# Packed attention with routed experts: another order in the first two batches of a one-core kernel

## The chip, the cores and the metric

One core of one Trainium2 chip. The time is the device time of one execution in microseconds (us), median of several runs. Engines are named as in the profile: PE (TensorE matmul) with PEld (its weight loads), DVE (VectorE), ACT (ScalarE), POOL (GpSimd), SP (SyncE, which here only issues DMAs). PE, DVE, ACT, POOL and SP each take their instructions in the order in which the program emits them; between engines only semaphores order the work.

## The reference

```python
def sm_attn(qq, kk, vv):
    s = scale * np.matmul(qq, kk.transpose(0, 1, 3, 2))
    a = np.exp(s - np.max(s, axis=-1, keepdims=True))
    a = a / (np.sum(a, axis=-1, keepdims=True) + 1e-09)
    return np.matmul(a, vv)
p_packed = sm_attn(p, k, v)              # 32 packed rows a head
out = sm_attn(q, p_packed, p_packed)     # 8 batches, 8 heads, 576 rows, 64 wide
x = out.transpose(0, 2, 1, 3).reshape(4608, 512)
logits = normalized(x) @ normalized(expert_emb).T / tau     # 8 experts
expert_idx = np.argmax(logits, axis=1)
gate_w = softmax(logits)[chosen]
out[mask] = gate_w[mask] * (np.maximum(x[mask] @ w1[e], 0) @ w2[e])   # for each expert e
```

q, k, v are 8 x 8 x 576 x 64, p is 8 x 8 x 32 x 64, w1 is 8 x 512 x 1024 and w2 is 8 x 1024 x 512, all fp32.

## The kernel before

The 8 batches run one after another, overlapped. For each batch the kernel packs keys and values into 32 rows a head (key scores, exponential, pack product), scores the queries against the packed rows (att2's softmax), and **guesses one expert for the whole batch** from the sum of the packed rows' logits (`guess`, the "choice": DVE's max and index, then a register load on the issuing engine). It loads that expert's w1 and w2 and runs the expert layer with it. Rows that another expert should have had are counted and redone at the end in a loop that is entered only if there are any.

The attention output is never formed: since it is attention weights (AT) times packed rows, the kernel multiplies packed rows by w1 once (`w1_rows`, `rows_w1`: the tile G) and the hidden layer is G times AT. The routing logits and squared norms come from a product of AT with the packed rows and their logits (ppx, `route`, L679). For the fp32r products tiles are split in a high and a low half (ACT casts the high half, POOL or DVE subtracts: `split`, `split_w2`, `split_g`), and each product is three passes (PASSES). For batch 0 the first half of the hidden layer runs unsplit on fp32.

`ffn` is one batch's expert layer as a generator that yields after each group of products: for batch 0 two w1 row products (L843) and 8 hidden products of the first half of the rows (L875), 8 of the second half, 8 steps of the last 64 rows (L902), then four row blocks c of 8 steps each (L920, three 128x512 products a step). After every yield a hand-written PLAN says what of other generators is emitted: "q" is the next part of `begin` (the head), "s" one step of batch 0's softmax (in the order ORDS), "G" one split of G, "a" one step of batch 1's attention (`att_main(1)`), "w" one split of a w2 tile, "r" one step of batch 0's `route`, "g" one step of batch 0's `gates`. PLAN's entry 0 is emitted before ffn starts, entry k after its k-th yield. When batch 1's routing is done (`x.lg` is set), `w1_rows(1)` is emitted between the steps of the last row block (c = AHEAD = 3).

ENG says for batch 0 which of the softmax steps S0 S1 N0 N1 L0 L1 (subtract the maximum, normalize, low half; for the two halves of the rows) and which of the four splits of G go to POOL ("p") rather than DVE ("v"). All later batches use DVE.

PSUM is kept in rotating banks: three "pf" (hidden and output products), two double "pb" (scores, routing, w1_rows), one "pc". Loads go out on SP's queue, some of the head's on ACT's, and for batch 1 on w1 and w2 on POOL's. An output copy (`store`, L1209: ACT scales by the gate) for the row block before is emitted at the third step of the next block; batch 0's first only at the second block.

Names: kn, vn, qn: the head's whole-tile loads of batch 0; kn1, ny: keys and packed queries of batch 1; wy: ny scaled and doubled (L1152); T, Tw: packed rows turned; flip: a DVE transpose of a key or query tile (L276, L281); rows_split: the high and low halves of ppx; L721: the counts.

Of the kernel before, what the change touches and what calls it, by code (L numbers as in the profile page):

```python
# [25 lines left out]
def kernel(  # L26
# [63 lines left out]
    def rsqrt(x, y, tag, eng=nc.vector):  # L90
# [3 lines left out]
            out=i, in0=x.bitcast(I32), scalar1=1, scalar2=None, op0=ALU.logical_shift_right  # L94
        )
        yield
        nc.vector.tensor_scalar(
            out=i, in0=i, scalar1=-1.0, scalar2=float(0x5F3759DF), op0=ALU.mult, op1=ALU.add
# [29 lines left out]
    def embeddings():  # L128

        emb_sb = sb.tile([E, DM], F32, name="emb_sb", tag="st", bufs=2)  # L130
# [300 lines left out]

    def att1(x, nat, tight=False):
# [3 lines left out]
        def queries():  # L436
            for r in range(NPR):
                x.qT[r] = flip(nat(NPR + r), False)
                yield
# [40 lines left out]
        def pack_slowly():  # L480
# [23 lines left out]
            yield from queries()  # L504
            yield from rows_main()

        def rows_main():
            for g in range(NG):
                rows_split(x, g)
# [5 lines left out]
            logits_split(x)  # L515
# [41 lines left out]
    def att2(x, after=None, first=False, b1=False):  # L557

        def eng(name, hf):
            i = ("S0", "S1", "N0", "N1", "L0", "L1").index(name + str(hf))  # L560
            return nc.gpsimd if first and ENG[i] == "p" else nc.vector

# [169 lines left out]
    def gates(x):  # L732
        lg, ss = x.lg, x.ss
        y = sm.tile([P, NC5], F32, name="gy", tag="gy", bufs=1)
        for n, _ in enumerate(rsqrt(ss, y, "g")):
            if n % 3 == 2:
                yield
# [91 lines left out]
    def ffn(x, store, late=False, after=None, end=False):  # L829
# [63 lines left out]
        for hf in range(2):  # L893
            for f in range(NF):
                if late and hf == 0 and f % 4 == 0:
                    yield from rows_w1(f // 4)
                yield from hidden(hf, f)
# [83 lines left out]
    def att_main(b):  # L981
# [7 lines left out]
        second = att2(x, keys_main(b + 1) if b else None, b == 0, b < 1)  # L989
        if b:  # L990
            for _ in range(3):
                yield next(second)
            load_w2(x, x.e, nc.gpsimd)
        yield from second
# [7 lines left out]
    def begin():  # L1002
# [9 lines left out]
        vn = [load_v(0, g, nc.scalar) for g in range(NG)]  # L1012
        nc.scalar.dma_start(itau, tau.broadcast_to([P, 1]))
        qn = [load_whole(q[0], g) for g in range(NG)]
        ny = sm.tile([P, NG, D], F32, name="pn", tag="pn")
        nc.sync.dma_start(ny, p[1].rearrange("(g h) j d -> (h j) g d", g=NG))
        kn1 = [load_whole(k[1], g) for g in range(NG)]
# [7 lines left out]
        def warm(n):  # L1025
# [3 lines left out]
            for _ in range(n):  # L1029
                nc.tensor.matmul(pt[:, :P], fill, fill, start=True, stop=True)  # L1030
# [10 lines left out]
        for g in range(NG):  # L1041
            x.s1[g] = turn_bank()
            for e in range(2):
                kt = flip(kn[g], True, e)
                for hf in range(2):
                    quarters(x.s1[g], pw[:, 1, g, e], kt, lambda c: head(g, c), hf, hf, e)
            if g == 0:
                for _ in range(3):
# [364 lines left out]
```

## Time and profile before

| | us |
|---|---|
| median of 3 runs | 460.34 |
| lowest and highest | 458.28, 461.69 |
| the profiled execution | 458.36 |
| its span, first to last instruction | 456.8 |
| PE busy | 434.9 (95%) |
| DVE busy | 302.9 (66%) |
| ACT busy | 204.9 (45%) |
| POOL busy | 142.6 (31%) |

Mean granted TensorE clock 0.988 of full speed. Busy shares are averages over stages with different limits, and matmuls are pipelined, so a busy PE is not PE at its peak. What the change touches lies in the first quarter of the span: the head (0 to 30 us), batch 0's expert layer (28 to 94 us) and batch 1's attention beside it.

### The profile page before, as it was taken

How to read it: one execution, taken by the hardware profiler on the slowest of the kernel's cores; microseconds unless marked ns; L12 is line 12 of the kernel's file. 1: busy time of each engine (PE TensorE's matmuls, PEld its weight loads, DVE VectorE, ACT ScalarE, POOL GpSimd, SP SyncE). 2: the span in 40 equal slices, each digit the busy share in tenths (PEclk: the TensorE clock that was granted, in tenths of full speed). 3: DMA queues.
4: the chain of work that ended last, by engine and by line, in shares of the span. 5: the costliest groups of instructions: out<-in, count | busy, mean ns of one | idle time of the engine just before them, and what ended most of it. 6: DMA issues, size and time to landing. Idle time of an engine off the chain costs nothing.

```text
span 456.8 us, 10781 instructions
## 1 busy us (share of the span) xinstructions
PE 434.9 (95%) x3926; PEld 345.6 (76%) x3927; DVE 302.9 (66%) x925; ACT 204.9 (45%) x478; POOL 142.6 (31%) x181
## 2 busy tenths in 40 slices
PE   8678999969999999999999999999999999999993
PEld 6556767739788886879788896879788796879783
DVE  4557588536895588847894589847895589635500
ACT  2356732536325661375325651375325652466210
POOL 2352744221621345041521336040531336033200
PEclk9999999979999999999999999999999999999998
DMA  8799168963596686866598665876597524711022
GB/s 255 273 263 275 40 181 295 291 187 106 142 374 197 162 222 204 291 191 181 154 361 229 169 190 199 295 200 180 156 347 229 151 54 154 268 30 24 13 53 47
DMA packets 39869, 87.12 MB, mean 191 GB/s; under 512 B 11769, under 2 KB 19193, under 8 KB 39809
## 3 DMA queue, kind: packets, MB, share of 16 engines
q1 hardware_dynamic: 31248, 56.52, 44.4%
q0 software_dynamic: 7840, 29.36, 17.5%
q8 instruction: 33, 0.54, 0.5%
q10 hardware_dynamic: 720, 0.48, 0.4%
q14 instruction: 28, 0.22, 0.2%
HBM read 76.89 MB, written 9.44 MB: 189 GB/s over the span
## 4 chain that ended last, share of the span: by engine, by line
PE 84%; DVE 6%; ACT 4%; DMA 2%; issue 1%; POOL 1%; SPq 0%; ACTq 0%; DVEq 0%; POOLq 0%
PE pf L920 36%; PE pf L875 22%; PE pf L902 6%; PE pt L679 6%; PE pt L253 3%; PE pt L808 2%; PE pt L374 2%; PE pt L357 2%; DMA pn<-in_p 1%; DMA out<-o 1%; DVE kt L276 1%; ACT p L342 1%; DVE hT L880 0%; DVE at L616 0%; PE pt L231 0%
## 5 line engine op out<-in xcount | busy, mean ns | idle before, releaser
L920 PE MATMUL pf<-w2s,hT 128*128 128x512 f32 (+1 forms) x792 | 189.2, 390 | 0.0
L920 PEld LDWEIGHTS pf<-w2s,hT 128*128 128x128 f32 x792 | 142.0, 188 | 38.3 <-issue 9.4
L784 POOL TENSOR_TENSOR w2s<-w2r,w2s 128x512 fp32r<-128x512 f32 x64 | 82.4, 1289 | 230.2 <-ACT w2s L783 226.3
L875 PE MATMUL pf<-AT,G 128*128 128x288 f32 x720 | 106.9, 302 | 0.7 <-DVE h L885 0.4
L875 PEld LDWEIGHTS pf<-AT,G 128*128 128x128 f32 x720 | 99.2, 191 | 6.7 <-issue 3.2
L880 DVE SCALAR_TENSOR_TENSOR hT<-pf,hT 128x224 fp32r<-128x224 f32 (+1 forms) x128 | 52.5, 415 | 36.3 <-ACT hT L879 36.1
L879 ACT ACTIVATE hT<-pf 128x224 fp32r<-128x224 f32 (+1 forms) x128 | 48.6, 385 | 49.5 <-PE pf L875 48.1
L783 ACT CAST w2s<-w2r 128x512 fp32r<-128x512 f32 x64 | 39.2, 616 | 2.1 <-issue 1.2
L1209 ACT ACTIVATE o<-pf,gate 128x512 f32<-128x512 f32 (+1 forms) x41 | 26.0, 635 | 30.6 <-PE pf L920 17.5
L695 ACT ACTIVATE at<-pt 128x512 f32<-128x512 f32 (+1 forms) x40 | 23.9, 597 | 34.1 <-DVE lg L688 33.2
L679 PEld LDWEIGHTS pt<-ppx,AT 128*128 128x128 f32 (+1 forms) x240 | 33.1, 177 | 5.3 <-ACT w2s L783 0.8
L679 PE MATMUL pt<-ppx,AT 128*128 128x264 f32 (+1 forms) x240 | 36.2, 287 | 0.4 <-ACT at L695 0.4
L902 PE MATMUL pf<-w2r,h 128*64 128x256 f32 x256 | 34.3, 390 | 0.0
L822 DVE TENSOR_TENSOR G<-pt,G 128x512 fp32r<-128x512 f32 x28 | 18.9, 690 | 17.9 <-ACT G L821 17.9
L688 DVE TENSOR_REDUCE lg<-pt 128x8 f32<-128x16 f32 (+1 forms) x40 | 6.6, 165 | 33.1 <-PE pt L679 33.0
L595 ACT ACTIVATE st<-st 128x576 f32<-128x576 f32 (+1 forms) x17 | 11.2, 660 | 31.1 <-DVE st L592 30.4
L902 PEld LDWEIGHTS pf<-w2r,h 128*64 128x64 f32 x256 | 15.6, 136 | 9.8 <-issue 4.1
L281 DVE STREAM_TRANSPOSE kt<-nat 128x576 f32<-128x576 f32 x28 | 21.3, 764 | 0.0
L773 POOL DMA_DIRECT2D w2r<-in_moe_w x28 | 19.7, 710 | 0.0
L746 ACT ACTIVATE lg<-lg 128x40 f32<-128x40 f32 x8 | 1.9, 237 | 39.6 <-DVE lg L742 39.6
L622 ACT CAST AT<-at 128x576 fp32r<-128x576 f32 x16 | 10.8, 673 | 19.6 <-DVE at L616 19.6
L821 ACT CAST G<-pt 128x512 fp32r<-128x512 f32 x28 | 15.9, 588 | 7.4 <-DVE G L822 4.8
(181 smaller groups left out, 483.8 us busy)
## 6 DMA issues: line engine op xcount, KB each, us to landing
nat<-in_q SPq DMA_DIRECT2D x112, 140.0 KB, 3.4
w1t<-in_moe_w POOLq DMA_DIRECT2D x14, 1024.0 KB, 6.7
w2r<-in_moe_w POOLq DMA_DIRECT2D x28, 512.0 KB, 9.9
nat<-in_k SPq DMA_DIRECT2D x96, 140.0 KB, 3.1
vn<-in_v SPq DMA_DIRECT2D x46, 192.0 KB, 4.5
out<-o SPq DMA_DIRECT2D x124, 64.0 KB, 2.2
nat<-in_k SPq DMA_DIRECT2D x4, 576.0 KB, 6.0
w1t<-in_moe_w SPq DMA_DIRECT2D x4, 512.0 KB, 5.7
```

The source lines that it names most:

```text
L281: nc.vector.transpose(kt.rearrange("p (c i) -> p c i", i=32), t)
L679: nc.tensor.matmul(pt[:r, 512 * g : 512 * g + XW], AT[:, a, g, c * P : c * P + r], x.ppx[:, m, g], start=(i == 0), stop=(i == 2),)
L695: nc.scalar.activation(scr[:r, :, : HB * D], ptv[:r, :, 0 : HB * D], AF.Square, accum_out=ss[:r, c : c + 1])
L773: queue.dma_start(t, w2e[:, 2 * i : 2 * i + 2, :])
L783: nc.scalar.copy(t[:, 0], raw)
L784: nc.gpsimd.tensor_tensor(out=t[:, 1], in0=raw, in1=t[:, 0].bitcast(F32), op=ALU.subtract)
L875: nc.tensor.matmul(pf[:, :HS], w, r, start=(n == 0), stop=(n == len(ops) - 1))
L879: nc.scalar.activation(hT[:, 0, f, cs], pf[:, :n], AF.Relu)
L880: nc.vector.scalar_tensor_tensor(out=hT[:, 1, f, cs], in0=pf[:, :n], scalar=0.0, in1=hT[:, 0, f, cs].bitcast(F32), op0=ALU.max, op1=ALU.su ...
L902: nc.tensor.matmul(pf[64 * hf : 64 * hf + 64, :256], h4[:, f], x.w2r[f // 2][:, f % 2, hf * 256 : hf * 256 + 256], start=(f == 0), stop=(f ...
L920: nc.tensor.matmul(pf[:, :w], hT[:, a, f, c * P : (c + 1) * P], x.w2s[f][:, m, at : at + w], start=(f == 0 and i == 0), stop=(f == NF - 1 ...
L1209: nc.scalar.activation(o[:, :w], pf[:, :w], AF.Copy, scale=x.gate[:, c : c + 1])
```

## The change

In the head: a tiny exponential (`seen`) is ACT's first instruction after the first load's issue, so the activation table is loaded there. The embeddings' Square is emitted before tau's load, rsqrt's first step after the third key flip, and the Newton steps later. The shift and multiply of rsqrt become one operation. The packed queries and keys of batch 1 (ny, kn1) are loaded behind the first exponentials, with ny in a buffer of the tag "p1". wy's scaling is emitted before batch 0's choice is drained rather than after batch 0's scores. The warm-up is 4 products of 512 columns instead of 13 of 128.

Around batch 0's layer: batch 1's key scores come behind the first w1 rows. The second w1 rows are emitted before the fourth hidden product instead of before the fifth. N1 and L1 of batch 0 go to POOL, and N0, N1 and L1 of batch 1 (ENG1). Batch 0's gate Newton steps go to POOL. Batch 1's query flips leave its attention generator and get a letter of their own ("d"); its choice, w1 load and query scores come directly after the packed rows, its w2 load and the splits of ppx after them; PLAN is rewritten.

```diff
         i = sm.tile(list(x.shape), I32, name="rq_i", tag=f"rq_i{tag}", bufs=1)
         nc.vector.tensor_scalar(
-            out=i, in0=x.bitcast(I32), scalar1=1, scalar2=None, op0=ALU.logical_shift_right
-        )
-        yield
-        nc.vector.tensor_scalar(
-            out=i, in0=i, scalar1=-1.0, scalar2=float(0x5F3759DF), op0=ALU.mult, op1=ALU.add
+            out=i, in0=x.bitcast(I32), scalar1=-0.5, scalar2=float(0x5F3759DF),
+            op0=ALU.mult, op1=ALU.add,
         )
         yield
...
     def embeddings():
 
+        seen = sm.tile([1, 1], F32, name="seen")
+        nc.scalar.activation(seen, ones[:1], AF.Exp)
         emb_sb = sb.tile([E, DM], F32, name="emb_sb", tag="st", bufs=2)
...
+    def all_queries(x, nat):
+        for r in range(NPR):
+            x.qT[r] = flip(nat(NPR + r), False)
+            yield
+
     def att1(x, nat, tight=False):
...
         def queries():
-            for r in range(NPR):
-                x.qT[r] = flip(nat(NPR + r), False)
-                yield
+            yield from all_queries(x, nat)
...
             nc.vector.tensor_copy(x.T, pu[:, 0 : NG * P])
-            yield from queries()
-            yield from rows_main()
-
-        def rows_main():
-            for g in range(NG):
-                rows_split(x, g)
             yield
             pt = pc.tile([P, 512], F32, name="pu", tag="pu")
             row_logits(x, pt)
             logits_out(x, pt)
             yield
-            logits_split(x)
...
-    def att2(x, after=None, first=False, b1=False):
+    def att2(x, after=None, first=False, b1=False, eng1="vvvvvv"):
 
         def eng(name, hf):
             i = ("S0", "S1", "N0", "N1", "L0", "L1").index(name + str(hf))
-            return nc.gpsimd if first and ENG[i] == "p" else nc.vector
+            return nc.gpsimd if (ENG if first else eng1)[i] == "p" else nc.vector
...
-        for n, _ in enumerate(rsqrt(ss, y, "g")):
+        for n, _ in enumerate(rsqrt(ss, y, "g", nc.gpsimd if x is bat[0] else nc.vector)):
...
             for f in range(NF):
-                if late and hf == 0 and f % 4 == 0:
-                    yield from rows_w1(f // 4)
-                yield from hidden(hf, f)
+                if late and hf == 0 and f == 0:
+                    yield from rows_w1(0)
+                if late and hf == 0 and f == 3:
+                    ahead, now = rows_w1(1), hidden(hf, f)
+                    for part in (ahead, now, ahead):
+                        next(part)
+                        yield
+                    yield from now
+                    drain(ahead)
+                else:
+                    yield from hidden(hf, f)
...
-        second = att2(x, keys_main(b + 1) if b else None, b == 0, b < 1)
+        second = att2(x, keys_main(b + 1) if b else None, b == 0, b < 1, ENG1 if b == 1 else "vvvvvv")
         if b:
             for _ in range(3):
                 yield next(second)
             load_w2(x, x.e, nc.gpsimd)
+            if b == 1:
+                yield
+                assert hasattr(bat[0], "lg")
+                for g in range(NG):
+                    rows_split(x, g)
+                    yield
+                logits_split(x)
         yield from second
...
         vn = [load_v(0, g, nc.scalar) for g in range(NG)]
+        next(emb_gen)
         nc.scalar.dma_start(itau, tau.broadcast_to([P, 1]))
         qn = [load_whole(q[0], g) for g in range(NG)]
-        ny = sm.tile([P, NG, D], F32, name="pn", tag="pn")
-        nc.sync.dma_start(ny, p[1].rearrange("(g h) j d -> (h j) g d", g=NG))
-        kn1 = [load_whole(k[1], g) for g in range(NG)]
...
-                nc.tensor.matmul(pt[:, :P], fill, fill, start=True, stop=True)
+                nc.tensor.matmul(
+                    pt, fill, fill.unsqueeze(1).broadcast_to([P, 4, P]), start=True, stop=True
+                )
...
                 kt = flip(kn[g], True, e)
+                if g and not e:
+                    next(emb_gen)
...
-            if g == 0:
-                for _ in range(3):
-                    next(emb_gen)
...
         key_exp(x, 1)
+        ny = sb.tile([P, S], F32, name="ny", tag="p1", bufs=2)[:, : NG * D]
+        ny = ny.rearrange("p (g d) -> p g d", g=NG)
+        nc.sync.dma_start(ny, p[1].rearrange("(g h) j d -> (h j) g d", g=NG))
+        kn1 = [load_whole(k[1], g) for g in range(NG)]
+        next(emb_gen)
+        next(emb_gen)
         p1_evac(x, 0, pt, 0)
         nc.vector.reciprocal(itau, itau)
-        next(emb_gen)
         key_sum(x, 0)
...
         nc.scalar.copy(x.Tw, pu[:, : NG * P])
+        wy = sb.tile([P, 2, NG, 2 * D], F32, name="wy", tag="w2s", bufs=NF)
+        nc.gpsimd.tensor_scalar(
+            out=wy[:, 0].rearrange("p g (t d) -> p g t d", t=2),
+            in0=ny.unsqueeze(2).broadcast_to([P, NG, 2, D]),
+            scalar1=SCALE, scalar2=None, op0=ALU.mult,
+        )
         drain(g_guess)
...
-    WARM = 13
+    WARM = 4
...
-    ENG = "pppvpvppvp"
+    ENG = "ppppppppvp"
+    ENG1 = "vvppvp"
...
     PLAN = (
-        "qsssqsssssssqsqssqsssqs", "s", "s", "G", "s", "G", "s", "s", "s", "sG",
-        "G", "", "aq", "a", "aq", "as", "aq", "aws", "aqs", "awq",
-        "aw", "awr", "awr", "ar", "awr", "awr", "aw", "ar", "g", "gr",
-        "gr", "gr", "ga", "ga", "gra", "gr", "gra", "ra", "a", "a",
-        "a", "a", "a", "a", "ga", "a", "a", "aa", "a", "a",
-        "aa", "a", "aa", "a", "aa", "aa", "aa", "aa", "aa", "aa",
+        "qsssqsssssssqsqssssss", "qqs", "s", "s", "sG", "", "G", "", "s", "s",
+        "sG", "a", "aG", "aq", "a", "aqs", "aq", "aws", "aqs", "awq",
+        "aw", "awr", "adwr", "adr", "adwr", "adwr", "aw", "ar", "ag", "agr",
+        "agr", "agr", "ga", "ga", "gra", "gr", "gra", "ra", "a", "a",
+        "a", "a", "a", "a", "ga", "a", "aa", "a", "aa", "a",
+        "aa", "a", "aa", "a", "aa", "a", "aa", "a", "aa", "aa",
         "aa",
     )
...
+        asked = all_queries(bat[1], nat_main(1))
...
+                elif c == "d":
+                    next(asked, None)
```

(wy's scaling stood further down, right before its own transposes, in the same words.)

## Rows read from the trace of the kernel before

**Rows 1.** Waits of PE, whole span: us in total, times, longest us.

```profile
PE pt L253 <- DVE cnt L726: 3.7, 1, 3.7
PE pf L1159 <- POOL wy L1152: 1.9, 1, 1.9
```

**Rows 2.** Windows near 100 us: busy per engine, granted clock, DMA share, GB/s.

```profile
97.00:98.00 1.00, 0.00 (x0) 0.00 (x0) 0.59 (x1) 0.37 (x1) 0.00 (x0) 0.98 0.53 125
...
104.00:105.00 1.00, 1.00 (x6) 1.00 (x6) 0.12 (x1) 0.55 (x3) 0.00 (x0) 0.60 0.31 77
```

**Rows 3.** Timeline, 72 to 112 us: start, us, engine, line, [idle before <-releaser].

```profile
99.08 2.15 PE L253 MATMUL pt<-kt,pw 64*32 64x288 f32 x24 [3.71 <-DVE cnt L726]
...
101.16 5.86 PE L875 MATMUL pf<-AT,G 128*128 128x288 f32 x30
```

**Rows 4.** The timeline, 0 to 20 us.

```profile
1.22 5.34 PE L1030 MATMUL pf<-fill 128*128 128x128 f32 x26 [1.22 <-DVE mask L72]
...
5.64 1.28 ACT L134 ACT_TABLE_LOAD   x1 [5.51 <-DMA pn<-in_p]
...
6.54 4.35 PE L231 MATMUL pt<-kt,pw 32*32 32x288 f32 x64
6.93 0.63 ACT L134 ACTIVATE esq<-emb_sb 8x512 f32<-8x512 f32 x1
```

**Rows 5.** The timeline, 20 to 48 us.

```profile
22.43 0.67 POOL L592 TENSOR_TENSOR st<-st,mx 128x288 f32<-128x288 f32 x1 [5.92 <-DVE mx L586]
...
30.21 4.15 PE L875 MATMUL pf<-at,g 128*128 128x288 f32 x16 [0.68 <-ACT g L855]
...
35.41 1.42 PE L843 MATMUL pf<-w1t,tw 64*32 64x512 f32 x16 [1.06 <-DVE hT L880]
...
41.75 3.62 PE L875 MATMUL pf<-AT,G 128*128 128x288 f32 x24
```

**Rows 6.** The timeline of POOL, 47 to 76 us.

```profile
49.39 1.44 POOL L627 TENSOR_TENSOR AT<-at,AT 128x576 fp32r<-128x576 f32 x1
...
59.12 2.53 POOL L784 TENSOR_TENSOR w2s<-w2r,w2s 128x512 fp32r<-128x512 f32 x2 [0.66 <-ACT w2s L783]
61.65 1.44 POOL L268 TENSOR_TENSOR ppx<-pp,ppx 128x256 fp32r<-128x256 f32 x2
...
70.22 1.76 POOL L765 DMA_DIRECT2D w1t<-in_moe_w  x2 [2.83 <-DMA nat<-in_k]
71.97 2.83 POOL L773 DMA_DIRECT2D w2r<-in_moe_w  x4
```

**Rows 7.** The timeline, 48 to 72 us, PE and DVE.

```profile
52.50 0.65 PE L902 MATMUL pf<-w2r,h 128*64 128x256 f32 x4
...
61.62 1.66 PE L920 MATMUL pf<-w2s,hT 128*128 128x512 f32 x6
...
68.75 0.22 DVE L550 TENSOR_SCALAR sel<-ecol,gi 1x8 f32<-1x8 f32 x1
...
70.52 0.85 DVE L581 STREAM_TRANSPOSE st<-pt 128x288 f32<-128x288 f32 x2 [1.55 <-PE pt L253]
```

**Rows 8.** The timeline, 0 to 20 us, POOL's small steps.

```profile
8.16 0.18 POOL L107 TENSOR_TENSOR rq_t<-rq_h,rq_i 8x1 f32<-8x1 f32 x1 [0.18 <-DVE rq_i L97]
...
9.24 0.18 POOL L107 TENSOR_TENSOR rq_t<-rq_h,ery 8x1 f32<-8x1 f32 x1
```

**Rows 9.** The timeline, 72 to 112 us, DVE and PE.

```profile
75.58 0.69 DVE L592 TENSOR_TENSOR st<-st,mx 128x576 f32<-128x576 f32 x1
...
81.72 0.76 DVE L627 TENSOR_TENSOR AT<-at,AT 128x576 fp32r<-128x576 f32 x1 [0.74 <-ACT AT L622]
...
90.27 1.95 PE L808 MATMUL pt<-w1t,T 64*32 64x512 f32 x32
```

**Rows 10.** The timeline of PE, 62 to 84 us.

```profile
70.36 13.57 PE L920 MATMUL pf<-w2s,hT 128*128 128x512 f32 x57
83.77 0.40 PE L679 MATMUL pt<-ppx,AT 128*128 128x264 f32 x2
```

More of the change, by code (lines that the diff above doesn't have):

```diff
@@ L1150, in begin @@
         yield
-        wy = sb.tile([P, 2, NG, 2 * D], F32, name="wy", tag="w2s", bufs=NF)
-        nc.gpsimd.tensor_scalar(
-            out=wy[:, 0].rearrange("p g (t d) -> p g t d", t=2),
-            in0=ny.unsqueeze(2).broadcast_to([P, NG, 2, D]),
-            scalar1=SCALE, scalar2=None, op0=ALU.mult,
-        )
         pu = bank()
```

## The prediction

> **What bounds the kernel now.** I read the page first: TensorE (PE) is busy almost throughout and its granted clock dips in one slice only, a little past 90 us. So time is lost where PE stands still, and the next view is the list of PE's waits. Its longest is 3.7 us before key scores of batch 2 (L253), the next 1.9 us before the transposes of the scaled packed queries wy (L1159) [rows 1]; neither has a like after 100 us. The windows show that the first wait costs more than itself: PE stands from 95.37 (99.08 less 3.71), the clock falls from full (2.4 GHz) to half (1.2) at about 97.96, and is full again at 104.8 [rows 2, 3]. As a mark I take the start of batch 1's second hidden product, 101.16, plus half of the 3.64 us that still run at half clock: **103.0**. Behind it PE works on without a wait in rows of the same kind, and the change leaves that work nearly as it is; so what the change is worth is how far it moves this mark. The third view is the timeline up to it, read engine by engine, because each engine takes its instructions in program order.
>
> **The head, 0 to 42 us.** The table load moves in front of the embedding load, the Square in front of tau's load, and the shift of rsqrt behind the third key flip. PE goes through the 64 key-score instructions in 4.35 us from 6.54 almost without a gap [rows 4], so an earlier last flip buys at most some 0.2 us; I take nothing. The warm-up goes from 26 instructions of 128 columns (5.34 us, 0.205 each) to 8 of 512. At the same rate one takes 0.82 us and PE is free for key scores at 7.8 instead of 6.54; at twice the rate at 4.5, before the first flip is there. So the cost lies between 0 and 1.25 us; I take **+0.4**, nearer to the low end, because the last of the eight fall into the stretch after 6.5 us, where PE ran the key scores at full pace. The Trainium skill ("ScalarE: Activation LUTs", What ACT_TABLE_LOAD costs) adds a drain of about 1.38 us to the 1.28 us of the load. Here the Square begins at 6.93, right where the load ended (5.64 + 1.28) [rows 4]; no drain shows. By the page the embedding load would go out that much later, the shift would hold up the last key flip, and I would add up to 1 us; the sum goes by the row.
>
> The scaling wy now stands on POOL before batch 0's shifts, and its source is loaded behind the first exponentials instead of far ahead. POOL stood idle for 5.9 us before the first shift [rows 5], so the 1.9 us wait goes: **-1.9**. ACT's key copies and the first exponential come behind that product in order, so both inputs of the first hidden product move with it. On SP the packed rows of batch 1 now wait for the buffer of the first exponentials, batch 1's keys and w1's issue stand behind them, and w1 waits for the first choice anyway; the keys would eat the gain if they landed after 22 us. On ACT's queue two of the six value loads go out some 1.5 us later (table load 1.28, a tiny exponential); the pack products come only after the last exponential, so I cost that at nothing.
>
> First half of the hidden layer: from 30.21 to 41.75, 11.5 us [rows 5]. Its 8 products take 1.04 each (4.15 for four), 8.3 in all, and the second w1 rows 1.4; the rest is waiting, above all for PSUM banks that DVE frees late. Now these rows go before the fourth product, and N1 and L1 leave DVE. DVE still does T1 before it frees the first bank, so one wait of about 0.1 to 0.4 remains: 9.8 us, **-1.7**. Cover for POOL's longer line: S1, N1 and two G splits like POOL's w2s step, 1.27 each, and L1 1.44 [rows 6], 6.5 us from about 28 with pauses between; the second half begins at about 38.5.
>
> Sum of the head: +0.4 - 1.9 - 1.7 = **-3.2 us**, between -0.6 (rival 3) and -4.
>
> **The choice and its loads.** PLAN entry k runs after the k-th yield of batch 0's ffn: 21 to 28 go with the L902 products, 29 to 36 with the first row block of L920, 37 to 44 with the second, and so on. Counting batch 1's "a" steps: the choice goes from entry 36 to 26, the first unpack from 39 to 32, the first routing product from 55 to 51. L902 ran from 52.50 to 61.62 [rows 7], its five steps with a routing product at 1.5 us each; it now starts at 49.3. The choice is issued at 49.3 + 5 x 1.5 = 56.8; DVE has the last query flip and a reduce to finish and then its own six small steps, some 1.5 us: sel ends at about 58.3. Two PE waits are new: the query scores need both banks, which routing's last chunk frees only after an ACT pass (0.6, an estimate by DVE's passes of 0.7), and that chunk waits for DVE behind a flip (0.4, half a pass).
>
> Now POOL. Its first w1 issue came 1.25 us after sel (68.97 to 70.22) [rows 6, 7], so now at 59.55. Behind it in POOL's order stand: two w1 issues 1.76, the eighth w2s step 1.27, four w2r issues 2.83, two ppx splits 1.44 [rows 6], and, new on POOL, batch 0's gate steps: 13 small operations. On POOL four such steps took 1.07 (8.16 to 9.24) [rows 8], so 13 take 3.5. Together 10.8 us: the square root is done at **70.4**. DVE's multiply by it stands in front of batch 1's first unpack. So that unpack, which leads batch 1's softmax, cannot begin before about 71.25 (four small DVE steps of 0.2, as sel's), where before it began at 70.52 [rows 7], though PE is ahead by then. From first unpack to the end of the second shift it was 5.75 us (70.52 to 76.27) [rows 7, 9]; six gate steps of 0.2 that used to lie ahead now lie between, 1.2 more: 78.2, and the second exponential, a pass like DVE's 0.7, ends on ACT at about 79.0.
>
> Who waits: batch 0's first output copy needs the gate and is queued on ACT behind that exponential (entry 39 holds the shift and exponential, and the copy comes after it). It is half a pass and ends at 79.5. It frees the PSUM bank that the third row block needs. PE starts the second block at 70.36 - 3.2 + 1.0 (new waits) - 0.4 (two waits inside the first block that go) = 67.8, at 0.235 an instruction (13.57 / 57 less its end [rows 10]) it ends at 73.4, and then **PE stands for 6.1 us**. The clock fell in the wait of 3.7 us, so I let it fall in this one, and be full again 5.7 us after the restart as it was then (99.08 to 104.8) [rows 2, 3]: 12 of the 21 instructions up to the routing run at 0.47, 9 at 0.235: routing begins at 87.3. Batch 1's attention is ready sooner: 11.96 us after the unpack before (82.48 less 70.52) [rows 7, 9], plus 1.2 for the gate steps and 0.7 for L1 (1.44 on POOL, 0.76 on DVE [rows 6, 9]; N0 and N1 lie beside other DVE steps), that is 85.1. So the moves in ENG1 are hidden behind PE, with 2.2 us to spare, and cost one for one beyond that.
>
> From routing to the mark: 27 L920 instructions 6.35; five routing products 3.7 (83.77 to 90.27 less 12 instructions of L920); w1 rows 1.9 [rows 9, 10] and 1.0 of wait for the last routing bank; key scores 1.1 (half of 2.15 at half clock [rows 3]), first hidden product and counts 1.2. Sum 15.3, the mark is at **102.6 to 102.7** against 103.0. The 3.7 us wait goes, since all w1 rows are now split before the last stores, but another has taken its place. What one operation less in every rsqrt saves on DVE is hidden beside PE.
>
> **Result.** 458.36 us for the profiled execution (span 456.8 and 1.56 around it), less 0.3: **458**. That execution is 2 us below the median of the three runs, 460.34, and equals the fastest; so by medians the same change reads 460, and the range covers both ways of reading.
>
> **Rivals.** (1) *The gate steps are not held up.* If POOL hands out the six load issues (4.6 us) without keeping its arithmetic waiting, the root is done at 65.8 instead of 70.4. Then the copy ends at 74.9, PE stands for 1.5 us, in which I let the clock hold as it did through the 1.9 us wait, routing waits for the attention until 80.5, and the mark is 95.8, 7.2 us ahead: **451**; with no wait at all routing begins at 78.4 and the time is 449. Against it: before, the six issues stand on POOL end to end, and count as its busy time [rows 6]. For it: no row shows arithmetic queued behind an issue. (2) *It does less than it says*: the earlier choice brings loads nobody waits for, and the gains of the head end at the third row block. That is my forecast's own reading, at 458, and has its chance. (3) *Slower.* In the head POOL's line S1, N1, G, G, L1 is one queue, and the second half of the hidden layer waits for its end. If each step waits for its ACT copy, L1 ends near 41, the second half starts where it did less 0.6, all later times slip by 2.6 and the mark is 105.2: **460.6**. It decides from L1 ending after about 38.8; each microsecond later costs one.
>
> **How the numbers follow.** Forecast 0.45, rival 1 0.35, rival 3 with late warm-up 0.20. A measurement of this kernel can tell about 1%, 4.6 us. Rival 1 is faster by over 1%, and so is a small part of the forecast's case (POOL done 3 us earlier): 0.40. Of rival 3 little over half would read as slower by over 1% with all bounds on the bad side: 0.12. The rest, 0.48, is within. The range goes from rival 1's 449 to 462, rival 3 with 1.25 for the warm-up.
>
> **What the changed profile would show.** Right: no wait before L1159; L1030 ending near 7; in the chain DVE's gate product waiting for POOL near 70; PE waiting for an ACT output copy (or the pf bank) near 73 to 80 with the clock down behind; no 3.7 us wait at L253. Wrong: batch 1's first unpack at 64 to 67 (rival 1), or the second half of the hidden layer starting after 40 with POOL as the releaser (rival 3). The weakest step is POOL's queue: one issue more or less in front of the gate steps moves the end by its own length.

## The result and the profile after

The changed kernel takes **454.41 us** (median of 4 runs, 453.98 to 455.36) against 460.79 in the same session (4 runs, 458.28 to 461.69): a ratio of 0.987, with a 95% interval of 0.983 to 0.992. The forecast was 458, the range 449 to 462. The profiled execution took 454.63 us (span 453.0), so against the one that the forecast started from (458.36) the change is worth 3.7 us, against the median 6.4. Why these differ is a finding of its own, below.

PE's waits, whole span (the first numbers are us in total, times, longest us). Those of [rows 1] are gone; one of 5.4 us stands in their place, and one of 1.1 us for T is new:

```profile
PE pf L923 <- ACT o L1223: 5.4, 1, 5.4
...
PE pf L870 <- ACT T L1194: 1.1, 1, 1.1
```

The timeline of the head. Answering to [rows 4]: the table load begins 4.24 us sooner, the warm-up ends as before (6.60 for 6.56), and key scores take 3.47 us where they took 4.35. Answering to [rows 5] and the first of [rows 7]: the two halves of the hidden layer and L902, now L905:

```profile
1.22 5.38 PE L1038 MATMUL pf<-fill 128*128 128x512 f32 x8 [1.22 <-DVE mask L72]
1.40 1.28 ACT L128 ACT_TABLE_LOAD   x1 [1.27 <-PEq L1409]
2.69 0.20 ACT L128 ACTIVATE seen<-ones 1x1 f32<-1x1 f32 x1
6.54 3.47 PE L230 MATMUL pt<-kt,pw 32*32 32x288 f32 x64
...
16.27 2.16 PE L1093 MATMUL pf<-ident,nat 128*128 128x128 f32 x18
...
19.96 0.44 PE L1173 MATMUL pf<-ident,wy 128*128 128x128 f32 x2
...
25.47 0.75 PE L870 MATMUL pf<-at,g 128*128 128x288 f32 x2
...
35.90 1.18 PE L870 MATMUL pf<-AT,G 128*128 128x288 f32 x6
...
38.47 1.87 PE L870 MATMUL pf<-AT,G 128*128 128x288 f32 x12 [1.14 <-ACT T L1194]
...
47.87 0.65 PE L905 MATMUL pf<-w2r,h 128*64 128x256 f32 x4
```

In the kernel before, the 18 query turns (L1093 here, L1079 there) were broken by a stall of 1.37 us, whose releaser the profile gives as "issue", that is, nothing that it shows:

```profile
18.68 1.83 PE L1079 MATMUL pf<-ident,nat 128*128 128x128 f32 x15 [1.37 <-issue]
```

The timeline of the middle, 55 to 100 us: POOL's queue, the gate product on DVE (L733), the first unpack (L576), the second exponential and the output copy on ACT (L590, L1223), PE's row blocks, the routing (L674) and the mark (L870):

```profile
57.56 1.75 POOL L760 DMA_DIRECT2D w1t<-in_moe_w  x2 [0.32 <-issue]
59.33 1.29 POOL L779 TENSOR_TENSOR w2s<-w2r,w2s 128x512 fp32r<-128x512 f32 x1
...
61.50 2.93 POOL L768 DMA_DIRECT2D w2r<-in_moe_w  x4 [0.38 <-issue]
...
61.62 10.07 PE L923 MATMUL pf<-w2s,hT 128*128 128x512 f32 x42
...
68.54 0.20 POOL L114 TENSOR_TENSOR gy<-rq_t,gy 128x5 f32<-128x5 f32 x1
68.77 0.17 DVE L733 TENSOR_TENSOR gy<-gy,ss 128x5 f32<-128x5 f32 x1 [6.86 <-POOL gy L114]
69.52 0.84 DVE L576 STREAM_TRANSPOSE st<-pt 128x288 f32<-128x288 f32 x2
...
75.95 0.68 ACT L590 ACTIVATE st<-st 128x576 f32<-128x576 f32 x1 [2.64 <-DVE st L587]
76.54 0.46 ACT L1223 ACTIVATE o<-pf,gate 128x256 f32<-128x256 f32 x1
77.05 7.92 PE L923 MATMUL pf<-w2s,hT 128*128 128x512 f32 x21 [5.36 <-ACT o L1223]
84.81 0.89 PE L674 MATMUL pt<-ppx,AT 128*128 128x264 f32 x6
...
99.22 1.98 PE L870 MATMUL pf<-AT,G 128*128 128x288 f32 x13
```

This is the chain of the forecast, link by link: POOL hands out six loads, all ahead of the last 11 of the 13 gate steps, DVE waits 6.86 us for the end of these, the first unpack follows, the output copy stands behind the second exponential, and PE stands from 71.69 to 77.05. The clock fell in that wait. The windows (PEclk is the number behind the five engines) have it at half from before the restart to about 83:

```profile
76.00:77.00 1.00, 0.00 (x0) 0.00 (x0) 0.04 (x1) 0.99 (x2) 0.92 (x1) 0.66 0.04 16
77.00:83.00 6.00, 5.96 (x14) 4.71 (x15) 4.85 (x10) 1.93 (x3) 2.38 (x2) 0.50 0.10 25
83.00:84.00 1.00, 1.00 (x5) 0.78 (x5) 1.00 (x3) 0.00 (x0) 0.65 (x3) 0.93 0.37 86
```

The mark, the second hidden product at full clock, stands at 99.22 where it was 103.0: 3.8 us, as the two spans differ (456.8 and 453.0). Behind it nothing is won or lost.

### The profile page after: what moved, and what is told of

Read it like the earlier page. It is cut to its first block, busy times and chain, and to the rows that moved or that the text cites. A ratio compares the mean times of both kernels' runs of the same rounds, so it can differ in the third digit from the quotient of the medians.

```text
span 453.0 us, 10735 instructions
## 1 busy us (share of the span) xinstructions
PE 435.5 (96%) x3908; PEld 343.3 (76%) x3909; DVE 295.8 (65%) x901; ACT 204.2 (45%) x479; POOL 152.2 (34%) x199
## 4 chain that ended last, share of the span: by engine, by line
PE 87%; DVE 4%; POOL 2%; ACT 2%; DMA 2%; issue 2%; SPq 0%; ACTq 0%; POOLq 0%; DVEq 0%
PE pf L923 38%; PE pf L870 23%; PE pf L905 6%; PE pt L674 6%; PE pt L252 3%; PE pt L803 3%; PE pt L373 2%; PE pt L356 2%; DMA emb_sb<-in_moe_expert_emb 1%; DMA nat<-in_k 0%; DVE mx L581 0%; PE pf L1093 0%; PE pf L838 0%; POOL w2r L768 0%; DVE st L576 0%
## 5 line engine op out<-in xcount | busy, mean ns | idle before, releaser
L923 PE MATMUL pf<-w2s,hT 128*128 128x512 f32 (+1 forms) x792 | 191.5, 394 | 5.4 <-ACT o L1223 5.4
L923 PEld LDWEIGHTS pf<-w2s,hT 128*128 128x128 f32 x792 | 144.2, 191 | 44.5 <-issue 8.9
L870 PE MATMUL pf<-AT,G 128*128 128x288 f32 x720 | 105.7, 299 | 1.4 <-ACT T L1194 1.1
L870 PEld LDWEIGHTS pf<-AT,G 128*128 128x128 f32 x720 | 97.7, 188 | 7.0 <-issue 2.8
L1223 ACT ACTIVATE o<-pf,gate 128x512 f32<-128x512 f32 (+1 forms) x41 | 25.9, 634 | 24.8 <-PE pf L923 17.8
L674 PEld LDWEIGHTS pt<-ppx,AT 128*128 128x128 f32 (+1 forms) x240 | 33.1, 177 | 4.6 <-ACT at L690 0.8
L674 PE MATMUL pt<-ppx,AT 128*128 128x264 f32 (+1 forms) x240 | 36.0, 286 | 0.3 <-ACT at L690 0.3
L905 PE MATMUL pf<-w2r,h 128*64 128x256 f32 x256 | 34.6, 391 | 0.0
L817 DVE TENSOR_TENSOR G<-pt,G 128x512 fp32r<-128x512 f32 x28 | 18.8, 690 | 15.3 <-ACT G L816 15.3
L590 ACT ACTIVATE st<-st 128x576 f32<-128x576 f32 (+1 forms) x17 | 11.2, 660 | 36.3 <-DVE st L587 33.7
L905 PEld LDWEIGHTS pf<-w2r,h 128*64 128x64 f32 x256 | 15.5, 136 | 10.2 <-issue 4.7
L280 DVE STREAM_TRANSPOSE kt<-nat 128x576 f32<-128x576 f32 x28 | 21.4, 766 | 0.0
L617 ACT CAST AT<-at 128x576 fp32r<-128x576 f32 x16 | 10.8, 674 | 20.2 <-DVE at L611 20.2
L275 DVE STREAM_TRANSPOSE kt<-nat 128x576 f32<-128x576 f32 x28 | 19.2, 737 | 0.0
```

The lines of the kernel that those rows point to most:

```text
L280: nc.vector.transpose(kt.rearrange("p (c i) -> p c i", i=32), t)
L674: nc.tensor.matmul(pt[:r, 512 * g : 512 * g + XW], AT[:, a, g, c * P : c * P + r], x.ppx[:, m, g], start=(i == 0), stop=(i == 2),)
L870: nc.tensor.matmul(pf[:, :HS], w, r, start=(n == 0), stop=(n == len(ops) - 1))
L905: nc.tensor.matmul(pf[64 * hf : 64 * hf + 64, :256], h4[:, f], x.w2r[f // 2][:, f % 2, hf * 256 : hf * 256 + 256], start=(f == 0), stop=(f ...
L923: nc.tensor.matmul(pf[:, :w], hT[:, a, f, c * P : (c + 1) * P], x.w2s[f][:, m, at : at + w], start=(f == 0 and i == 0), stop=(f == NF - 1 ...
L1223: nc.scalar.activation(o[:, :w], pf[:, :w], AF.Copy, scale=x.gate[:, c : c + 1])
```

## The experiments

**1. Gate steps back on DVE.**

```diff
-        for n, _ in enumerate(rsqrt(ss, y, "g", nc.gpsimd if x is bat[0] else nc.vector)):
+        for n, _ in enumerate(rsqrt(ss, y, "g")):
```

> The changed kernel with batch 0's gate steps back on DVE, all else as changed. Theory A (POOL's queue holds the gate steps, they hold DVE's first unpack of batch 1, and PE stands for that): the first unpack begins near 61.5 instead of 69.5 us, the 5.4 us wait before the third row block goes, no fall of the clock near 76, routing of batch 1 begins near 76.6 instead of 84.8, time 446 to 448. Rival B (the attention of batch 1 or the output copy would be late anyway, DVE being full): first unpack earlier, but PE still stands 3 us or more before routing, time 452 to 455.

Measured: **449.14 us** (448.40 to 449.56; ratio 0.977, 0.974 to 0.981). In PE's timeline the wait for the output copy falls from 5.36 to 1.16 us, and the 21 instructions behind it take 5.17 us at full clock (granted 1.00 from 70 to 85 us), where they took 7.92:

```profile
72.53 5.17 PE L923 MATMUL pf<-w2s,hT 128*128 128x512 f32 x21 [1.16 <-ACT o L1223]
77.53 0.89 PE L674 MATMUL pt<-ppx,AT 128*128 128x264 f32 x6
```

So the gate steps on POOL, behind its load issues, cost the changed kernel 5.3 us. The first unpack came at 64.99, not at 61.5: DVE's steps were themselves slow, five of them 0.60 to 2.29 us instead of 0.17 (run 3 has more on this).

**2. Batch 1's w2 loads behind the splits of ppx**, gate steps on POOL.

```diff
-            load_w2(x, x.e, nc.gpsimd)
+            if b > 1:
+                load_w2(x, x.e, nc.gpsimd)
             if b == 1:
                 yield
...
                 logits_split(x)
+                load_w2(x, x.e, nc.gpsimd)
```

> The changed kernel with batch 1's four w2 load issues on POOL moved behind the splits of ppx and their logits, so behind batch 0's gate steps. Theory A: each microsecond taken from POOL ahead of the root is a microsecond earlier for the first unpack: root at 65.8 instead of 68.8, copy at 73.6 instead of 76.5, PE waits 1.9 instead of 5.4 us; 450 to 451 if the clock holds in that wait, 452.5 if it falls. Rival (issues do not keep arithmetic waiting): root at 68.8 as before, 454 to 455.

Measured: **450.30 us** (449.51 to 450.87; ratio 0.980, 0.975 to 0.985). PE's timeline shows the wait shrunk by the 2.9 us of the four issues and a little more:

```profile
73.89 6.66 PE L923 MATMUL pf<-w2s,hT 128*128 128x512 f32 x21 [2.12 <-ACT o L1225]
```

The four issues alone cost 4.1 us: some 3 as a wait, and the rest mostly in the 21 instructions behind it, 6.66 instead of 7.92, since the clock stands at half for some 3.4 us instead of 6.8. The expectation had 452.5 for a fall of the clock; it fell, but for a shorter time.

**3. Both of these.**

> The changed kernel with batch 0's gate steps on DVE and batch 1's w2 loads behind the splits of ppx: neither step of the square root waits for POOL, and no load issue lies beside DVE's gate steps. Theory A (the six issues, not POOL's arithmetic, cost the 5.4 us wait, and their neighbourhood slowed DVE's steps in the run with the gates alone): DVE's small steps take 0.2 to 0.3 us each, the first unpack of batch 1 starts at 61.5 to 63, PE waits for the first output copy by less than 0.5 us, and the time is 446.5 to 448.5. Theory B (DVE's steps are slow beside any work of POOL): the steps stay at 0.6 to 0.75, first unpack near 65, and the time is that of the better one alone, 449 to 450.

Measured: **448.78 us** (447.72 to 449.83; ratio 0.975, 0.972 to 0.978), the fastest median but one here, and no better than run 1 beyond the scatter. PE's wait for the copy is 0.26 us, but the first unpack began at 64.22, not by 63. The timeline shows why: one small DVE step, the first of rsqrt, takes 2.99 us. In the kernel before the same step took 0.16 us (at 63.53), beside an idle POOL. Here it ends as the first of the two ppx splits does:

```profile
58.17 2.99 DVE L93 TENSOR_SCALAR rq_i<-ss 128x5 int32<-128x5 int32 x1
...
59.14 1.29 POOL L779 TENSOR_TENSOR w2s<-w2r,w2s 128x512 fp32r<-128x512 f32 x1
...
60.37 1.44 POOL L267 TENSOR_TENSOR ppx<-pp,ppx 128x256 fp32r<-128x256 f32 x2
...
64.22 0.84 DVE L576 STREAM_TRANSPOSE st<-pt 128x288 f32<-128x288 f32 x2
```

Theory A was right on the issues and wrong on DVE. This step makes the unpack late, but with PE's wait for the copy down to 0.26 us, no more than that can be won at this place.

**4. The output copy ahead of the second exponential**: PLAN entries 39 and 40 changed from one "a" each to none and two.

```diff
-        "agr", "agr", "ga", "ga", "gra", "gr", "gra", "ra", "a", "a",
-        "a", "a", "a", "a", "ga", "a", "aa", "a", "aa", "a",
+        "agr", "agr", "ga", "ga", "gra", "gr", "gra", "ra", "a", "",
+        "aa", "a", "a", "a", "ga", "a", "aa", "a", "aa", "a",
```

> The changed kernel with one step of batch 1's softmax (second shift and exponential) emitted one entry later, so that batch 0's first output copy stands before that exponential in ACT's order. Theory A: the copy ends near 73.8 instead of 77.0 and PE waits 2.1 instead of 5.4 us there, but batch 1's attention is still ready only near 83.5, so a wait of some 4.8 us appears before routing: 453 to 455. Rival (only ACT's order holds PE): no second wait, 449 to 451.

Measured: 454.79 us (453.30 to 455.38; ratio 0.989, 0.984 to 0.994), the changed kernel's time. The wait for the copy falls to 2.1 us, and PE stands in the routing instead, 0.4 us for the attention and 3.6 us for a bank. That bank waits for a reduce on DVE at 84.60, which is queued behind the late attention's last steps and batch 2's four key flips. PE's waits:

```profile
PE pt L674 <- ACT at L690: 3.9, 2, 3.6
PE pf L923 <- ACT o L1223: 2.1, 1, 2.1
```

The order on ACT alone is not the cause: the late square root holds DVE's whole line.

**5. The old warm-up** (26 matmul records of 128 columns instead of 8 of 512).

```diff
-                nc.tensor.matmul(
-                    pt, fill, fill.unsqueeze(1).broadcast_to([P, 4, P]), start=True, stop=True
-                )
+                nc.tensor.matmul(pt[:, :P], fill, fill, start=True, stop=True)
...
-    WARM = 4
+    WARM = 13
```

> The changed kernel with the warm-up of the kernel before (13 products of 128 columns instead of 4 of 512). In the kernel before PE stood 1.4 us among the query turns with nothing that the profile names; in the changed kernel it does not. Theory C (the warm-up does not matter): no such wait, 454 to 455. Rival D (it goes with the 36 fewer PE instructions ahead of it): the 1.4 us stand again near 17 us, 455 to 456.

Measured: 455.43 us (ratio 0.991, 0.988 to 0.995), 1.0 above the changed kernel. But its 10 runs spread from 452.60 to 458.02, where the changed kernel's 4 spread by 1.4. The profiled one is the fastest, without a stall in its head. So the median is rival D's and the trace is theory C's, and this run settles neither. The profile doesn't show what spreads the runs: the half clock behind the wait for the copy also lasted less there (from 76.2 to 79.6 us, against 76.3 to 83.1). See run 8.

**6. The old order of the hidden layer's first half**: second w1 rows before the fifth product, N1 and L1 on DVE.

```diff
-                if late and hf == 0 and f == 0:
-                    yield from rows_w1(0)
-                if late and hf == 0 and f == 3:
-                    ahead, now = rows_w1(1), hidden(hf, f)
...
-                else:
-                    yield from hidden(hf, f)
+                if late and hf == 0 and f % 4 == 0:
+                    yield from rows_w1(f // 4)
+                yield from hidden(hf, f)
...
-    ENG = "ppppppppvp"
+    ENG = "pppvpvppvp"
```

> The changed kernel with the first half of batch 0's hidden layer as it was: second w1 rows before the fifth product, N1 and L1 of batch 0 on DVE. Theory A (the prediction's term of 1.7 us): the first L905 instruction starts 1.7 us later than in the changed kernel, near 49.5 instead of 47.6 to 48.1, and the time is 455.5 to 456.5, because everything behind (choice, gate steps, first output copy) hangs on that start. Theory B (the wait of 1.14 us for T before the second half takes up part of it): L905 near 48.3, no wait for T, and a time within 0.7 us of 454.4. Theory C (N1 and L1 on POOL were the cost, not the gain): L905 no later than 47.9.

Measured: 455.84 us (455.43 to 456.97; ratio 0.991, 0.988 to 0.994), 1.4 above the changed kernel. PE's timeline:

```profile
37.28 1.06 PE L870 MATMUL pf<-AT,G 128*128 128x288 f32 x6 [0.15 <-DVE hT L875]
...
39.90 1.86 PE L870 MATMUL pf<-AT,G 128*128 128x288 f32 x12 [1.14 <-ACT T L1186]
...
49.22 0.65 PE L897 MATMUL pf<-w2r,h 128*64 128x256 f32 x4
```

The second half begins at 37.28 against 35.90, and the wait for T is as long: it moves with its place and takes up nothing. The last products of the stage start 1.35 us later. Theory A, at 1.4 instead of 1.7 by the medians; of the 1.35, 0.43 lie ahead of the first hidden product (25.90 against 25.47), which the edit doesn't touch, so the stretch itself is 0.95 longer.

**7. The kernel before with wy's scaling moved**, nothing else.

```diff
         nc.scalar.copy(x.Tw, pu[:, : NG * P])
+        wy = sb.tile([P, 2, NG, 2 * D], F32, name="wy", tag="w2s", bufs=NF)
+        nc.gpsimd.tensor_scalar(
...
-        wy = sb.tile([P, 2, NG, 2 * D], F32, name="wy", tag="w2s", bufs=NF)
-        nc.gpsimd.tensor_scalar(
```

> The kernel before with one edit: the scaling of the packed queries (wy) stands where the changed kernel has it, ahead of batch 0's shifts; loads, choice and PLAN as before. Theory A (the term of 1.9 us): no wait of PE before the wy transposes; the first w1 rows start near 26.5 (28.43 before), L902 near 50.6 (52.50), and the time falls by 1.9 us, to 458 to 459 as a median. Theory B (another input of the first hidden product is late as well): the wait goes, but less than 1 us of it reaches L902. Apart from both: the stall of 1.37 us without a releaser among the query turns (18.68) shows again if it belongs to the kernel before, and does not if it is an accident of one execution.

Measured: 458.10 us (454.16 to 458.41; ratio 0.994, 0.991 to 0.997). The wait goes, the median falls by 2.4 (460.51 beside it), and yet L902 of the profiled execution starts at 52.29, only 0.2 sooner. What ate the rest there is PE's stall without a releaser among the query turns, which came again (1.14 us), this time with a fall of the clock (mean granted 0.72 from 18 to 24 us, where it was 1.00):

```profile
18.92 3.32 PE L1079 MATMUL pf<-ident,nat 128*128 128x128 f32 x15 [1.14 <-issue]
```

So it is no accident of one execution. Alone this run doesn't settle the size; run 9 does.

**8. The kernel before once more.**

> The kernel before, unchanged, for a second profile. If its executions differ by what the clock does behind the two stalls (among the query turns and before the key scores of batch 2), this one shows the same two stalls, 1.1 to 1.4 and 3 to 4 us, with another stretch at half clock, and its time follows: near 458 without a fall in the head, near 461 with one. If the stall among the query turns is an accident, it is not there.

Measured: 460.18 us. The stall is there, 1.70 us long; behind it 15 turns take 3.36 us (the changed kernel's 18 take 2.16), and L902 starts at 54.82, 2.3 us later than in [rows 7]. PE's timeline, and the windows with the clock at 0.50:

```profile
16.78 0.49 PE L1079 MATMUL pf<-ident,nat 128*128 128x128 f32 x3
18.97 3.36 PE L1079 MATMUL pf<-ident,nat 128*128 128x128 f32 x15 [1.70 <-issue]
...
26.30 0.44 PE L1159 MATMUL pf<-ident,wy 128*128 128x128 f32 x2 [1.87 <-POOL wy L1152]
...
54.82 0.65 PE L902 MATMUL pf<-w2r,h 128*64 128x256 f32 x4
```

```profile
17.00:18.00 1.00, 0.27 (x3) 0.14 (x2) 0.40 (x3) 0.63 (x2) 0.00 (x0) 0.75 0.07 28
18.00:24.00 6.00, 5.03 (x47) 3.45 (x46) 1.75 (x3) 1.17 (x2) 0.00 (x0) 0.50 0.74 237
```

So the kernel before has executions of at least two kinds. In the one that the forecast read, the clock held through the stall (458.36); in this one it falls (460.18, near the median). These 1.8 us are most of the 2.7 by which the medians differ more than the profiles. Its 54 executions beside the runs fit this: the 28 with a mean granted clock of 0.982 or less took 460.1 to 462.9 us, the other 26 455.6 to 460.8. Which stall makes the clock low in each of them, their times don't say.

**9. The kernel before with wy moved and the loads of batch 1's packed queries and keys at their new place.**

```diff
-        nc.sync.dma_start(ny, p[1].rearrange("(g h) j d -> (h j) g d", g=NG))
-        kn1 = [load_whole(k[1], g) for g in range(NG)]
...
         key_exp(x, 1)
+        nc.sync.dma_start(ny, p[1].rearrange("(g h) j d -> (h j) g d", g=NG))
+        kn1 = [load_whole(k[1], g) for g in range(NG)]
```

> The kernel before with the early scaling of wy and, in addition, the loads of batch 1's packed queries and keys behind the second exponential, as the changed kernel has them. Theory A (these loads, issued ahead of everything else on SP's queue, make PE's nameless stall of 1.1 to 1.4 us among the query turns): no stall there, L902 near 49.3 to 50 (52.50 before, 52.29 with the scaling alone), the median at 456 to 457. Theory B (the stall belongs to something else of the old head): it stays at 1.1 to 1.4 us and L902 starts at 50.6 or later.

Measured: 457.26 us (453.98 to 458.01; ratio 0.993, 0.990 to 0.996). Theory B: the stall stays, at 1.70 us, and the clock falls behind it too. That makes this profile a twin of run 8's up to wy, and their difference is wy's price: 54.82 less 52.92 is **1.90 us** (PE's timeline).

```profile
19.00 3.36 PE L1079 MATMUL pf<-ident,nat 128*128 128x128 f32 x15 [1.70 <-issue]
...
24.40 0.44 PE L1159 MATMUL pf<-ident,wy 128*128 128x128 f32 x2
...
52.92 0.65 PE L902 MATMUL pf<-w2r,h 128*64 128x256 f32 x4
```

**10. The changed kernel with those loads at their old place** (the reverse edit, ny in its own buffer again).

> The changed kernel with the loads of batch 1's packed queries and keys at their old place, right behind batch 0's queries. Theory A (loads make the stall): PE stalls by 1.1 to 1.4 us among the query turns near 17 and L905 starts near 49, the time is 455.5 to 456.5. Theory B (they don't): no stall, L905 at 47.5 to 48.2, 454 to 455.

Measured: 454.28 us (453.10 to 455.00; ratio 0.987, 0.983 to 0.991), the changed kernel's time, without a stall: its 18 query turns run through in 2.16 us from 17.09. L905 does start late in this profile, at 48.96, where theory A had put it, but not by a stall: the warm-up ran to 8.00 us and PE then waited 0.8 us for the embeddings' norm on POOL. In the time the loads' place is worth nothing that can be measured.

**11. ENG1 all on DVE** in the changed kernel.

```diff
-    ENG1 = "vvppvp"
+    ENG1 = "vvvvvv"
```

> The changed kernel with all softmax steps of batch 1 on DVE (N0, N1, L1 back from POOL). Theory A (the prediction: hidden, with about 2 us to spare behind the late output copy): PE's wait of 5.4 us for the first output copy stays, batch 1's attention is ready within 1 us of where it was (83.5), and the time is within 1 us of 454.4. Theory B (DVE is full there and the three steps of 0.7 us lie on the attention's chain): attention ready at 85 or later, a PE wait for it of 0.5 to 1.5 us before the routing, and a time of 455 to 456.

Measured: 454.38 us (453.65 to 455.01; ratio 0.987, 0.983 to 0.992), the same. The attention is ready at 81.91 (L622 on DVE) instead of 83.52 (on POOL), 1.6 us sooner, and PE's wait of 5.4 for the copy stays. Hidden, as forecast.

**12. The same on top of run 3**, where the copy no longer covers it.

> The changed kernel with the gate steps on DVE, batch 1's w2 loads behind the splits of ppx, and all softmax steps of batch 1 on DVE. Theory A (with the output copy out of the way the attention is next, and what POOL's slower N0, N1 and L1 cost it then counts one for one): the attention is ready 1 to 1.6 us sooner, the routing starts 0.3 to 0.7 us sooner than with POOL (76.75), and the time is 448.0 to 448.5 against 448.8. Theory B (PE's own work sets the start of the routing already): the same time as with POOL, within 0.2 us.

Measured: 448.56 us (448.05 to 449.82; ratio 0.976, 0.973 to 0.979), 0.2 less than run 3 and not to be told from it. The routing begins 0.5 sooner (76.24 against 76.75), but the whole head had, too (L905 at 47.16 against 47.69), and the sooner routing then waits longer for its bank: its reduce on DVE is queued behind batch 2's four key flips, as the timeline of the three engines shows.

```profile
76.73 2.71 DVE L275 STREAM_TRANSPOSE kt<-nat 128x576 f32<-128x576 f32 x4
79.37 0.21 DVE L683 TENSOR_REDUCE lg<-pt 128x8 f32<-128x16 f32 x2
79.60 0.60 ACT L690 ACTIVATE at<-pt 128x512 f32<-128x512 f32 x1 [3.48 <-DVE lg L683]
...
80.34 1.00 PE L674 MATMUL pt<-ppx,AT 128*128 128x264 f32 x6 [1.77 <-ACT at L690]
```

Neither theory: the attention gains, and DVE's order takes it back. Runs 1, 3 and 12 are all faster than both kernels, by 5.3 to 5.9 us against the changed one; among the three nothing can be told apart, since the kernel before itself read 459.4 to 460.8 as a median on the four occasions.

## Why the prediction was right, step by step

**The mechanism** was the forecast's: POOL's queue holds the gate steps, these hold the first unpack, the copy behind the exponential holds PE, and the clock falls. Runs 1 and 2 show it by taking out either half of the queue, run 4 by moving the wait to the next in line. Rival 1, the gate steps not held up, is what run 1 makes of the kernel: the forecast gave it 449 to 451, it took 449.14. That this is so close is in part luck: the head was 1.4 us better than forecast, and PE still waited 1.16 us. Rival 3 is out: L1 of batch 0 ended on POOL at 34.89, against the 38.8 from which it would have decided.

**The sizes.** The mark came at 99.22 and not at 102.65, 3.4 us early:
- *The head*, -3.2 forecast, -4.6 measured (L902 from 52.50 to L905 at 47.87). The wy term was exact (1.90, run 9), the hidden order near (1.4 for 1.7, run 6). The term that was wrong is the **warm-up at +0.4**: it cost nothing here (1.22 to 6.60). In eight of the nine profiles with it, key scores end 1.3 to 1.5 us after the last key flip, as with the old one; in run 10's it ran to 8.00 and they ended 2.45 after it. Three terms were left out. The stall of 1.37 us in the profile of before, which I had read past because it had no releaser, went. Key scores were not bound by PE as I took them to be, but by the last flip: it ended 0.64 us sooner and they ended 0.9 sooner, not at the same time. And with batch 1's key scores behind the first w1 rows, waits of 0.90 and 0.68 us ahead of the first hidden product went, some 0.7 us from wy's transposes to that product. Against that, the wait of 1.14 us for T is new. The sum is that of one pair of executions: L905 starts between 47.2 and 49.0 in the nine profiles that have it, L902 at 54.82 in run 8.
- *The choice*: sel ended 8.2 us after L905's start and not 9.0 (-0.8).
- *POOL's queue*: 57.56 to 68.74 is 11.2 us, forecast 10.8 (+0.3); the first issue came 1.5 after sel, not 1.25 (+0.2).
- *Unpack to restart*: the second exponential ended 7.1 us after the unpack, not 7.75, and the copy 0.37 behind it, not 0.5 (-0.8).
- *PE's wait* 5.4 for 6.1; the restart to the routing 7.76 for 7.8.
- *Routing to mark*: 14.4 for 15.3; the bank wait of 1.0 didn't come (-0.9). The 3.7 us for the routing products came out (84.81 to 90.63 less nine instructions of L923), but I had read them wrongly: the rows of before hold nine instructions of L920 there and not 12, which would have made them 4.4, with a wait of 0.41 among them.

The forecast that the choice brings "loads nobody waits for" held: it is 12.9 us sooner (sel at 55.85 for 68.75), and the first unpack behind POOL's queue only 1.0 (69.52 for 70.52).

**The base.** I noted that the profiled execution was 2 us under the median and let the range cover it. The reason was to be had from that profile: a stall in which the clock may fall or hold belongs to the execution, and a change that removes the stall gains more in the median than in that profile.

**What removed the stall** is not the loads (runs 9, 10). The trace points to PE's own program. The transfers list a queue of kind "instruction" with 33 packets, 0.54 MB in all, so 16 KB each, in the kernel before:

```profile
q8 instruction: 33, 0.54, 0.5%
```

In all four profiles of the old head PE stalls after the same instruction, the 219th matmul and 220th weight load (26 warm-up, 64 key scores, 126 up to the query turns, then 3 and 4 of these). The first such packet began between 16.2 and 16.6 us, took 1.0 to 1.1, and ended 1.2 to 1.4 before PE resumed. With the new warm-up 18 matmuls and as many weight loads fewer lie ahead, so PE comes to its 220th weight load behind all 18 turns, over a microsecond later. The wait stands at that count in the changed kernel too, only shorter, four weight loads into the next product (PE's weight loads):

```profile
18.35 0.14 PEld L1153 LDWEIGHTS pt<-spare,tw 64*32 64x32 f32 x4 [0.17 <-DVE spare L1145]
18.84 0.17 PEld L1153 LDWEIGHTS pt<-spare,tw 64*32 64x32 f32 x12 [0.34 <-issue]
```

Six of the nine profiles with that warm-up have it there, 0.34 to 0.66 us long, and in all six the weight loads go on 1.2 to 1.4 us after the first packet's end. In the other three, and in run 5, where with the old warm-up the packet ran at 14.3, 1.3 to 1.7 us from that end had passed when PE came to this count, and there is no wait. So the traces show a wait that goes by the count of PE's instructions and by a 16 KB packet, and a warm-up with fewer of them that puts more work ahead of it. That the packet holds PE's instructions and that bulk loads delay it is my reading. The kernel before with the new warm-up alone was not run, so what this is worth by itself is not shown.

The table load went as [rows 4] had it: it ended at 2.68, and the next activation began at 2.69. The Trainium skill ("ScalarE: Activation LUTs", What ACT_TABLE_LOAD costs) adds a drain of about 1.38 us; by that rule it would begin at 4.06, and the trace again doesn't agree: no drain shows behind the load.

## What to carry to other kernels

Before a small step is moved to an idle engine, list what that engine issues around it: a load issue (0.73 to 0.88 us here) is work like any other, and four of them ahead of a step that gates three engines cost 4.1 us here. A wait that is moved away from one place is worth its length only if the next wait in line is looked at too (runs 4 and 12). And a wait of PE "for nothing" in one profile deserves a second profile of the same kernel before it is left out of the sum.

## What was not expected of the hardware

- A small DVE step (L93, 128x5) took 0.16 us beside an idle POOL in the kernel before, and 2.29 (changed kernel), 2.29 (run 1) and 2.99 us (run 3) where POOL issued loads and ran splits; each time it ended within 0.1 us of the end of a POOL split. The first row is of the kernel before, the second of the changed kernel:

```profile
63.53 0.16 DVE L93 TENSOR_SCALAR rq_i<-ss 128x5 int32<-128x5 int32 x1
...
58.36 2.29 DVE L93 TENSOR_SCALAR rq_i<-ss 128x5 int32<-128x5 int32 x1
```

  The kernel before has it beside splits alone: its step L699 (128x40) took 1.09 us and ended at 61.69, POOL's split at 61.65. The Trainium skill ("SBUF — State Buffer", SBUF: two separate sides) says that DVE and GpSimd share a pair of ports by an exclusive lock, held for an instruction; on DVE's side it names operations in a two-port mode or with two inputs in SBUF. The trace agrees with a step that waits for a whole split; no run here shows in which mode the step ran. What held it in the first microsecond, when POOL only issued loads, is open: in run 1 two steps of 0.60 and 0.67 us also stand beside load issues alone (between 60.22 and 63.11), so splits are not all that slows DVE.
- PE can stall for 1.1 to 1.7 us at a fixed count of its instructions, 1.2 to 1.4 us after the end of a 16 KB packet of the queue "instruction" (four profiles). Whether the clock then falls (granted 0.50 from 18 to 24 us in run 8, 1.00 in the kernel before's first profile) goes with 2.3 us by L902.
